# A chunked attention and maxout kernel on one core: tile 0's q and k in two halves, a new order of the first list, new planned times

## The chip, the core and the metric

The kernel runs on one core of a Trainium2 chip. Its engines work side by side: TensorE (matmuls, PE in the rows, with its weight loads as PEld), VectorE (DVE), ScalarE (ACT), GpSimd (POOL), and SyncE (SP), which issues all loads and stores here. The metric is device time in microseconds (us), the median of several runs.

## What is computed

Attention over chunks of 64 positions, for 8 batches, 8 heads, 576 positions and a head size of 64, and behind it a layer that takes the largest of three products:

```
scores = q_c @ k_c.T / 8                     per chunk of 64
attn   = softmax(scores);  x = attn @ v_c    x: 4608 tokens x 512
h      = max(x @ w1, x @ w2, x @ w3)         512 -> 768
out    = h @ w_out                           768 -> 512
```

All in float32. q and k are drawn some 6.5 times larger than v.

## The kernel before, in words

The 4608 tokens are 36 tiles of 128. **Tiles 0 to 3** are the first group, tiles 4 to 7 the second, and tiles 8 to 35 four units of 6, 8, 8 and 6. A product of float32 matrices is made of three matmuls on high and low parts (lines 175 to 177, and 587 in the units). In the units the big products are made with seven smaller products in place of eight, so sums and differences of operands ("mixing") are prepared for weights and for x.

**The steps of a tile** (`plain_steps`, line 205 on) have short names, by which the orders are written: `q` (load q and k, line 213), `v` (load v, 217), `S` (32 score matmuls, 228), `mx` (maximum, VectorE, 233), `sub` (subtract it, VectorE, 238), `exp` (ScalarE, 242), `sum`, `eps`, `rec` (VectorE, 183, 186, 189), `nrm` (normalise, 192, GpSimd or VectorE), `T` (transpose by TensorE, 254), `at` (copy of it, ScalarE, 259), `V` (32 value matmuls, 266), `xh` and `xl` (high part on ScalarE, 273, low part on VectorE, 277), or `x` (plain copy, 280). Score banks of even and odd tiles lie side by side in one tile of PSUM; buffers of e alternate between two, those of sums too.

**A piece of weights** jw (`piece`, line 122 on) is a 512 KB load `W` (142), then `A` and `B` on ScalarE (151, 156), `C` on VectorE (160), `X` (164), `H` (high part, ScalarE, 167) and `Y` (low part, 170); a `p` behind the name puts X or Y (or nrm, hl) on GpSimd.

**The first list** (`FIRST`, line 42 on) writes out the order of the first group by hand; each engine takes its own names in that order. `i7` is seven idle matmuls on zeros (756). `h00a` is the hidden product of piece 00 with the first 256 columns (tiles 0 and 1), `b` the second, `f` all 512; it is 12 matmuls and needs H and Y of its piece and xh and xl of its tiles. `F` takes the result out of PSUM, `hh` and `hl` split the hidden values, `P` and `O` are the output products and their stores, `K` stores plain weights for the units, `M` starts the planner.

**Behind M a planner sets the order.** Its clock `now` starts at -10 and moves by a step (0.6815 for three matmuls of 512 columns) with each piece of TensorE's work. `plan(at, pe, fn)` files an operation for a time, and `passed` releases what is due, in order of time; one with a `pe` moves the clock. These times set only the order in which the program gives operations to the engines. In the second group's 72 hidden steps, four insertions (`first_tiles`, `insertion`, line 857 on) put V and S of two tiles, their softmax (offsets in `SOFTMAX`) and their T between the steps; `begins` shifts the softmax of each of the two and `behind` says how long after that its transpose is due. `stores` (line 883) files the mixing of weights (GpSimd sums into `c`, high part 389, low part 392, store 406) in nine rounds of 6.94 from `MIX`. Behind the 72 steps come 24 output steps, during which `operands` (510) makes the operands X1 to X7 of unit 0, from `OPERANDS` on: differences (499), high parts on ScalarE (504), low parts on VectorE (508). Operands 4 and 5 share a room for their differences. Then unit 0 begins; its products (587) are copied out by ScalarE (601) and summed.

## Time and profile before

| what | value |
|---|---|
| median of 3 runs | 613.57 us (613.57 to 613.94) |
| the profiled execution | 613.93 us, its span 612.2 us |
| TensorE busy | 604.1 us (99%), 5107 matmuls |
| VectorE, GpSimd, ScalarE busy | 428.4 (70%), 294.0 (48%), 271.8 us (44%) |
| granted TensorE clock | 1.00 over the span |
| moved by DMA | 161.26 MB, mean 263 GB/s |

Times in the rows count from the first instruction. In a timeline each line has start, duration, engine, line of the kernel, operation, what it writes and reads, and how many instructions it merges; in brackets how long the engine stood idle before it and what ended that. A busy TensorE is not one at its peak, as ends of matmuls are modelled; starts are the surer number.

### The profile page before, as it was taken

The numbers are of one execution on the slowest core, as the hardware profiler recorded it, in microseconds if no ns is written. First come the engines' busy times: TensorE is split into PE (matmuls) and PEld (weight loads), VectorE is DVE, ScalarE is ACT, GpSimd is POOL, SyncE is SP. The second block draws the span as 40 slices with busy tenths as digits, with TensorE's granted clock in tenths as the row PEclk, the third lists the DMA queues.
The fourth block names the chain that finished last, engine by engine and source line by source line (L and its number), as shares of the span: only waits on it lengthen the run. The fifth ranks groups of instructions, "written<-read, shape, count | busy, mean of one in ns | idle before, by whom it ended". The sixth has DMA issues, their size and how long they took to land.

```text
span 612.2 us, 12724 instructions
## 1 busy us (share of the span) xinstructions
PE 604.1 (99%) x5107; PEld 526.0 (86%) x5107; DVE 428.4 (70%) x677; ACT 271.8 (44%) x483; POOL 294.0 (48%) x242
## 2 busy tenths in 40 slices
PE   8999999999999999999999999999999999999997
PEld 4888888877899999998888887888888888999997
DVE  5899834787657988794596859863868387375752
ACT  4898633444444554544252525432434252242440
POOL 3352699884257775454262624532534234242430
PEclk9999999999999999999999999999999999999999
DMA  8999729687989997889485848497565658977774
GB/s 318 385 337 307 238 103 357 231 308 276 346 290 311 358 356 267 283 303 360 175 294 172 279 152 287 144 331 285 174 204 205 200 172 265 325 247 243 241 233 177
DMA packets 54219, 161.26 MB, mean 263 GB/s; under 512 B 4880, under 2 KB 16144, under 8 KB 49168
## 3 DMA queue, kind: packets, MB, share of 16 engines
q1 hardware_dynamic: 54160, 160.45, 74.9%
q8 instruction: 40, 0.66, 0.4%
q14 instruction: 19, 0.16, 0.1%
HBM read 128.97 MB, written 31.46 MB: 262 GB/s over the span
## 4 chain that ended last, share of the span: by engine, by line
PE 77%; DVE 7%; POOL 6%; ACT 2%; issue 2%; DMA 1%; SPq 1%; POOLq 0%; ACTq 0%; DVEq 0%
PE pm L587 65%; POOL c L384 3%; PE pm L175 2%; PE pm L177 2%; PE pm L176 2%; POOL f L371 2%; DVE s L392 1%; PE y L266 1%; PE s L228 1%; DMA w<-s 1%; PE s L266 1%; ACT s L389 1%; PE y L228 1%; PE s L254 1%; DVE e L238 1%
## 5 line engine op out<-in xcount | busy, mean ns | idle before, releaser
L587 PE MATMUL pm<-X,ring 128*128 128x512 f32 (+1 forms) x1512 | 311.0, 364 | 0.3 <-ACT kept L601 0.3
L587 PEld LDWEIGHTS pm<-X,ring 128*128 128x128 f32 x1512 | 271.4, 188 | 30.6 <-ACT kept L601 0.7
L601 ACT COPY kept<-pm 128x384 f32<-128x384 f32 (+1 forms) x108 | 57.2, 534 | 139.2 <-PE pm L587 101.1
L587 PE MATMUL pm<-Y,ring 128*128 128x512 f32 (+1 forms) x504 | 103.2, 363 | 0.1
L587 PEld LDWEIGHTS pm<-Y,ring 128*128 128x128 f32 x504 | 90.6, 188 | 10.4 <-DVE Y L637 0.6
L611 POOL TENSOR_TENSOR kept<-kept 128x384 f32<-128x384 f32 (+1 forms) x36 | 45.5, 1263 | 79.9 <-ACT kept L601 79.8
L598 DVE TENSOR_TENSOR most<-pm,most 128x384 f32<-128x384 f32 (+1 forms) x72 | 44.8, 622 | 51.7 <-PE pm L587 50.3
L192 POOL TENSOR_TENSOR e<-e,sm 128x512 f32<-128x512 f32 x28 | 33.1, 1181 | 71.1 <-DVE sm L189 52.5
L175 PE MATMUL pm<-xh,wl 128*128 128x512 f32 (+1 forms) x156 | 59.8, 383 | 0.0
L177 PE MATMUL pm<-xh,wh 128*128 128x512 f32 (+1 forms) x156 | 58.3, 374 | 0.0
L176 PE MATMUL pm<-xl,wh 128*128 128x512 f32 (+1 forms) x156 | 58.2, 373 | 0.0
L607 POOL TENSOR_TENSOR kept<-kept 128x384 f32<-128x384 f32 (+1 forms) x24 | 29.7, 1236 | 57.6 <-DVE kept L604 49.1
L637 DVE TENSOR_TENSOR Y<-most,Y 128x384 fp32r<-128x384 f32 (+1 forms) x72 | 53.7, 761 | 3.4 <-ACT Y L634 3.2
L634 ACT CAST Y<-most 128x384 fp32r<-128x384 f32 (+1 forms) x72 | 40.1, 570 | 30.2 <-DVE most L598 15.9
L242 ACT ACTIVATE e<-e 128x512 f32<-128x512 f32 x36 | 22.7, 631 | 37.6 <-DVE e L238 37.5
L604 DVE TENSOR_TENSOR kept<-pm,kept 128x384 f32<-128x384 f32 (+1 forms) x36 | 22.3, 621 | 18.4 <-PE pm L587 15.2
L604 DVE TENSOR_TENSOR pm<-pm,kept 128x384 f32<-128x384 f32 (+1 forms) x48 | 30.1, 628 | 7.1 <-PE pm L587 5.7
L177 PEld LDWEIGHTS pm<-xh,wh 128*128 128x128 f32 x156 | 29.4, 188 | 5.4
L175 PEld LDWEIGHTS pm<-xh,wl 128*128 128x128 f32 x156 | 29.4, 188 | 5.1
L176 PEld LDWEIGHTS pm<-xl,wh 128*128 128x128 f32 x156 | 29.4, 189 | 4.7
L183 DVE TENSOR_REDUCE sm<-e 128x8 f32<-128x512 f32 x36 | 24.5, 680 | 8.2 <-ACT e L242 7.6
L371 POOL TENSOR_TENSOR f<-wh,wl 128x512 f32<-128x512 f32 x18 | 28.3, 1594 | 0.6
(112 smaller groups left out, 838.3 us busy)
## 6 DMA issues: line engine op xcount, KB each, us to landing
ring<-w SPq DMA_DIRECT2D x36, 1024.0 KB, 5.6
ring<-w SPq DMA_DIRECT2D x36, 768.0 KB, 5.5
ring<-wo SPq DMA_DIRECT2D x28, 768.0 KB, 4.7
buf<-in_qk SPq DMA_DIRECT2D x36, 512.0 KB, 6.4
buf<-in_vb SPq DMA_DIRECT2D x36, 256.0 KB, 4.9
w<-s SPq DMA_DIRECT2D x18, 512.0 KB, 4.0
out_t<-ao SPq DMA_DIRECT2D x16, 256.0 KB, 3.9
wo<-so SPq DMA_DIRECT2D x3, 1024.0 KB, 7.2
```

Of the source, the lines that this page charges most:

```text
L175: nc.tensor.matmul(out=o, lhsT=al, rhs=bh, start=first, stop=False)
L176: nc.tensor.matmul(out=o, lhsT=ah, rhs=bl, start=False, stop=False)
L177: nc.tensor.matmul(out=o, lhsT=ah, rhs=bh, start=False, stop=last)
L192: eng.tensor_tensor(out=e, in0=e, in1=sm.unsqueeze(2).broadcast_to([P, 8, 64]), op=ALU.mult)
L371: nc.gpsimd.tensor_tensor(out=st["f"][:, k], in0=wh[j][:, w].bitcast(F32), in1=wl[j][:, w].bitcast(F32), op=plus)
L587: nc.tensor.matmul(out=o[i], lhsT=a, rhs=b, start=new and k == 0, stop=last and k == 2, skip_group_check=i in banks_of_product)
L598: return lambda: nc.vector.tensor_tensor(out=M(k, c), in0=of(), in1=M(k, c), op=most)
L601: return lambda: nc.scalar.copy(out=kept(k), in_=o[i])
L604: return lambda: nc.vector.tensor_tensor(out=out(), in0=o[i], in1=kept(k), op=plus)
L611: (0.0, lambda: nc.gpsimd.tensor_tensor(out=kept(2), in0=kept(2), in1=kept(0), op=plus))],
L634: return lambda: nc.scalar.copy(out=y_room(i, jp)[:, 0, :half], in_=t[i]())
L637: return lambda: nc.vector.tensor_tensor(out=y_room(i, jp)[:, 1, :half], in0=t[i](), in1=y_room(i, jp)[:, 0, :half].bitcast(F32), op=minus)
```

## The change

q and k of a tile were laid out as all heads of q, then all of k. They are now laid out as heads 0 to 3 of q and k, then heads 4 to 7 of both, and tile 0 is loaded in two transfers of half the size. The hand-written list has a new order, with some X and Y moved between VectorE and GpSimd, and the planner's times have new values. The diff, without unchanged lines (the lists whole):

```diff
@@ -31,10 +31,10 @@
-SOFTMAX = (("mx", 0.93), ("sub", 1.87), ("exp", 3.09), ("sum", 3.8), ("eps", 4.34), ("rec", 4.95), ("nrm", 5.17))
+SOFTMAX = (("mx", 0.93), ("sub", 1.87), ("exp", 3.09), ("sum", 3.8), ("eps", 4.54), ("rec", 4.95), ("nrm", 5.17))
-OPERANDS = 0.94
-MIX = 0.52
+OPERANDS = 1.64
+MIX = 1.22
@@ -44,21 +44,26 @@
-i7 q0 q1 S0 i7 mx0 sub0 q2 exp0 sum0 W00 S1 A00 eps0 B00 S2 rec0 mx1 sub1 exp1 W02 nrm0p i2 C00 q3 mx2 X00p v0 i1 A02
-sum1 i8 T0 at0 S3 H00 V0 eps1 i3 rec1 sub2 nrm1p xh0 v1 mx3 exp2 T1 Y00p at1 i3 xl0 sum2 C02 V1 q4 eps2 rec2 sub3 B02
-W01 nrm2p v2 q5 xh1 X02p xl1 W10 S4 T2 exp3 A01 sum3 h00a v3 at2 eps3 rec3 V2 H02 nrm3 Y02 B01 C01 F00a W12 xh2 B10
-X01 mx4 sub4 T3 at3 H01 h02a A10 V3 Y01 S5 xh3 h01a A12 C10 W11 A11 xl3 B12 xl2 exp4 F01a F02a X10p W21 C12 W22 Z B11
-W20 hh0a W30 H10 A20 W31 Y10p h02b X12 mx5 A30 h00b q6 C20 C11 q7 B20 sum4 W42 hl0a H12 X11p Y12 X20 W32 H11 Y11 h01b
-F00b eps4 sub5 B21 H20 rec4 A21 B31 F01b F02b Y20p h10f C30 W40 B30 h12f A22 A31 C21 nrm4p exp5 C22 X30 X21 B22 h11f
-W51 H30 h20f W50 hh0b S6 C31 hl0bp H21 X31p X22 Y21 F10f H22 A32 F11f F12f v4 B51 Y30p H31 hh1f T4 h21f W41 B32 B50
-A40 Y31p sum5 mx6 A50 W62 eps5 B42 Y22p C40 h31f B40 at4 hl1f W60 C50 F20f C32 A41 X40 X32p K11 H40 F21f B41 Y40 h22f
-H32 Y32 X50 A51 C51 C41 A42 sub6 rec5 X51 H50 X41 Y50p h30f A60 h40f F22f W61 W65 W52 B62 C42 W64 H51 X42 exp6 h32f
-hh2f W63 H42 Y51 S7 H41 nrm5 B65 V4 hl2f C60 B60 Y41 F30f T5 v5 A52 X60p F31f K12 A62 F32f B52 hh3f Y42 H60 B61 C52
-hl3f F40f h41f h50f K20 sum6 C62 X52 mx7 A61 C61 xh4 F41f Y60 H52 h42f A65 X62 H62 F42f eps6 X61p Y52p v6 A64 Y62 h51f
-H61 hh4f A63 P30 Y61p P20 sub7 B63 C63 K00 rec6 exp7 hl4f P32 sum7 P31 F50f nrm6p P21 X63p at5 eps7 H63 Y63p rec7 P10
-xl4 nrm7p V5 K22 K01 B64 F51f K10 T6 xh5 h52f v7 at6 C64 P22 X64p C65 P00 xl5 T7 F52f H64 hh5f P23 X65p P01 hl5fp M
-at7 H65 P11 V6 V7 q8 q9 P12 xh6 xh7 xl6 P02 Y64 P13 xl7 Y65 P33 P34 P14 P35 P24 P03 P25 P04 K21 O2 P15 P05 K02 O0 O3
-O1
+q0 q1 i5 S0 mx0 i3 q2 S1 W01 mx1 sub0 exp0 i7 i2 v0 sub1 exp1 sum0 eps0 v1
+rec0 A01 W00 sum1 B01 S2 nrm0p mx2 i8 eps1 C01 A00 T0 rec1 at0 sub2 exp2 sum2 eps2 C00
+q3 B00 nrm1p i5 V0 T1 xh0 rec2 X01p S3 xl0 at1 nrm2p W10 H01 mx3 V1 Y01p sub3 A10
+xh1 exp3 X00p xl1 i1 sum3 T2 q4 B10 S4 eps3 v2 W02 rec3 h01a at2 q5 v3 V2 nrm3
+H00 A02 W12 Y00 T3 B02 xh2 C02 X02 at3 H02 h00a mx4 F00a W20 C10 Y02 V3 xh3 F01a
+S5 A12 B12 X10p xl3 W11 H10 xl2 C12 Z X12 B11 A11 h02a W21 W32 h00b Y10p F02a H12
+W22 sub4 C11 A20 hh0a C20 h02b W40 W30 exp4 hl0a B20 A21 h01b X20 B21 X11 W60 F00b W52
+W41 C21 Y12p sum4 eps4 H20 H11 B32 X21 B30 h10f Y11 F01b A32 Y20p A30 rec4 H21 C32 F02b
+hh0b C30 nrm4p mx5 hl0bp A22 Y21 B41 h12f W42 W63 v4 F10f q6 X32 C22 sub5 B22 h11f A42
+X22p W31 h20f h21f B40 X30 H32 Y32 S6 F11f H22 H30 T4 F12f B42 hh1f W51 mx6 A31 C42
+Y22p B52 X42 A40 exp5 C31 at4 Y30p W50 hl1f H42 h22f W61 Y42p A41 h30f B31 h32f F20f C41
+X31p A60 sub6 X41p F21f B51 H31 C40 Y31 H41 exp6 F22f sum5 h42f h31f hh2f sum6 A52 X40 Y41p
+B50 H40 eps5 B60 W62 A50 eps6 C60 B63 C52 hl2f X52p C50 rec5 q7 F30f Y40p A51 h41f h40f
+F31f F32f S7 B61 hh3f H52 K12 X60 C51 X51p W64 nrm5 B64 K01 X50 hl3f Y52 F40f A62 rec6
+F41f C62 F42f H50 V4 T5 xh4 nrm6p Y50 mx7 B62 A64 H51 X62p H60 hh4f xl4 v5 at5 h52f
+Y51 sub7 W65 Y60 exp7 A63 C64 h50f h51f sum7 H62 C63 eps7 X63p A61 P00 Y62 hl4f V5 T6
+C61 H63 F50f X61 F51f H61 K00 A65 rec7 F52f Y61p P20 P22 K11 hh5f v6 X64 P30 C65 P32
+P31 xh5 H64 K22 K20 at6 P21 Y63p nrm7p xl5 hl5fp P01 B65 v7 P10 P23 K10 T7 X65 M
+at7 H65 P11 V6 V7 q8 q9 P12 xh6 xh7 xl6 P02 Y64 P13 xl7 Y65 P33 P34 P14 P35
+P24 P03 P25 P04 K21 O2 P15 P05 K02 O0 O3 O1
@@ -208,9 +213,13 @@
-            st["r"] = att.tile([P, 2, 8, 64], F32, name="buf", tag=("raw", "kk", "aa")[t % 3] if t < 8 else ("raw", "kk")[t % 2],
+            st["r"] = att.tile([P, 2, 2, 4, 64], F32, name="buf", tag=("raw", "kk", "aa")[t % 3] if t < 8 else ("raw", "kk")[t % 2],
-            nc.sync.dma_start(out=st["r"], in_=qk[t])
+            if t == 0:
+                for k in range(2):
+                    nc.sync.dma_start(out=st["r"][:, k], in_=qk[t][:, 512 * k:512 * k + 512])
+            else:
+                nc.sync.dma_start(out=st["r"], in_=qk[t])
@@ -225,7 +234,7 @@
-                    nc.tensor.matmul(out=s[b, c, g, :], lhsT=r[a, 0, 2 * g + h, :], rhs=r[a, 1, 2 * g + h, :],
+                    nc.tensor.matmul(out=s[b, c, g, :], lhsT=r[a, g // 2, 0, g % 2 * 2 + h, :], rhs=r[a, g // 2, 1, g % 2 * 2 + h, :],
@@ -409,8 +418,8 @@
-                (0.12, sum_of(0, sums(1), a11, minus)), (4.07, sum_of(2, a11, a21, minus)),
-                (3.79, sum_of(3, a12, sums(0), minus)), (4.86, high), (5.79, low), (8.77, mixed)]
+                (2.32, sum_of(0, sums(1), a11, minus)), (4.07, sum_of(2, a11, a21, minus)),
+                (3.79, sum_of(3, a12, sums(0), minus)), (4.86, high), (5.79, low), (7.57, mixed)]
@@ -465,9 +474,9 @@
...
@@ -508,20 +517,20 @@
-            return [(0.0, high(1)), (0.39, low(1)), (2.71, mix(5, b12, b11, nc.vector)), (3.48, high(5)),
-                    (3.31, mix(6, b22, source[5], nc.vector)), (8.01, mix(7, b22, b12, nc.gpsimd)), (3.37, high(6)),
-                    (7.69, low(6)), (7.41, high(2)), (7.89, low(5)), (10.85, mix(4, b21, source[6], nc.gpsimd)), (7.67, low(2)),
+            return [(0.0, high(1)), (0.0, low(1)), (2.01, mix(5, b12, b11, nc.vector)), (3.83, high(5)),
+                    (3.31, mix(6, b22, source[5], nc.vector)), (8.21, mix(7, b22, b12, nc.gpsimd)), (3.37, high(6)),
+                    (7.49, low(6)), (7.06, high(2)), (7.89, low(5)), (12.35, mix(4, b21, source[6], nc.gpsimd)), (8.37, low(2)),
-            return [(1.17, high(3)), (2.45, low(3)), (0.47, high(4)), (1.08, low(4))]
+            return [(1.17, high(3)), (1.75, low(3)), (1.0, high(4)), (1.08, low(4))]
...
@@ -606,16 +615,16 @@
...
@@ -640,20 +649,20 @@
...
@@ -687,13 +696,13 @@
...
@@ -847,14 +856,14 @@
-            plan(at + 2.27, 0.0, lambda: steps(n)["at"]())
+            plan(at + 1.92, 0.0, lambda: steps(n)["at"]())
-            plan(at - loads + 0.38 * k, 0.0, lambda n=n: steps(n)["v"]())
-            plan(at + 1.41 + 0.58 * k, 0.0, lambda n=n: steps(n)["x"]())
+            plan(at - loads + 0.03 * k, 0.0, lambda n=n: steps(n)["v"]())
+            plan(at + 1.41 + 0.78 * k, 0.0, lambda n=n: steps(n)["x"]())
@@ -863,11 +872,11 @@
-        gap = (time - lead - 0.5) / (len(own) - 1)
+        gap = (time - lead - 0.0) / (len(own) - 1)
-            insertion(values, scores, now + lead + gap * i, 11.6, nc.gpsimd if last else nc.vector,
-                      (0.7, 4.6) if last else (0.2, 3.02), (10.9, 10.9) if last else (10.1, 9.4))
+            insertion(values, scores, now + lead + gap * i, 12.25, nc.gpsimd if last else nc.vector,
+                      (2.2, 3.9) if last else (0.0, 3.12), (11.25, 8.7) if last else (9.3, 9.4))
@@ -878,7 +887,7 @@
...
@@ -887,7 +896,7 @@
...
@@ -920,7 +929,7 @@
...
@@ -941,13 +950,13 @@
-              ("do", lambda: tiles(1, 4 * JT * STEP + span(0))), ("do", lambda: load(0, 0, 1.72, 1.35)), ("do", lambda: load(0, 1, 2.31, 5.13))]
+              ("do", lambda: tiles(1, 4 * JT * STEP + span(0))), ("do", lambda: load(0, 0, 2.02, 2.15)), ("do", lambda: load(0, 1, 2.31, 5.83))]
-        parts.append(("do", lambda u=u: operands(u + 1, 7.76)))
+        parts.append(("do", lambda u=u: operands(u + 1, 7.86)))
@@ -994,8 +1003,8 @@
-    qk, vb = (np.concatenate([a.transpose(0, 1, x, 2, y).reshape(NT, P, 512) for a in group], axis=2)
-              for group, x, y in (((q, k), 4, 3), ((v,), 3, 4)))
+    qk = np.stack([a.transpose(0, 1, 4, 2, 3).reshape(NT, P, 2, 256) for a in (q, k)], axis=3).reshape(NT, P, 1024)
+    vb = v.transpose(0, 1, 3, 2, 4).reshape(NT, P, 512)
```

## Rows read from the trace of the kernel before

**Rows 1.** Waits of TensorE: us in total, times, longest us

```profile
PE x L266 <- DMA buf<-in_vb: 1.3, 1, 1.3
PE s L228 <- DVE e L238: 0.7, 1, 0.7
PE y L266 <- ACT xs L259: 0.4, 1, 0.4
PE pm L587 <- ACT kept L601: 0.3, 1, 0.3
PE s L254 <- DVE e L192: 0.3, 1, 0.3
```

**Rows 2.** Line 213, its first two loads: duration ns, first and last start; landing

```profile
L213 SPq DMA_DIRECT2D buf<-in_qk x2: 388/402/416, 0.7 to 1.2; - x2
...
DMA to landing us min/median/max: 3.9/4.3/4.7
```

**Rows 3.** Timeline of the first 25 us; columns as told above

```profile
4.70 0.56 PEld L228 LDWEIGHTS s<-buf 64*64 64x64 f32 x32 [0.99 <-DMA buf<-in_qk]
...
5.47 0.69 DVE L233 TENSOR_REDUCE mx<-s 128x8 f32<-128x512 f32 x1 [4.07 <-PE s L228]
...
7.58 0.69 DVE L183 TENSOR_REDUCE sm<-e 128x8 f32<-128x512 f32 x1 [0.70 <-ACT e L242]
...
14.35 0.69 DVE L277 TENSOR_TENSOR xl<-x,xh 128x512 fp32r<-128x512 f32 x1 [1.16 <-ACT xh L273]
...
16.90 0.69 PE L228 MATMUL s<-buf 64*64 64x64 f32 x32 [0.67 <-DVE e L238]
...
16.92 0.69 DVE L277 TENSOR_TENSOR xl<-x,xh 128x512 fp32r<-128x512 f32 x1
...
17.96 0.36 PE L175 MATMUL pm<-xh,wl 128*128 128x256 f32 x1
...
18.30 0.59 ACT L259 COPY xs<-tp 128x512 f32<-128x512 f32 x1 [0.20 <-PE tp L254]
...
18.79 0.62 ACT L167 CAST wh<-ao 128x512 fp32r<-128x512 f32 x1
...
19.56 0.69 PE L266 MATMUL x<-xs,buf 64*64 64x64 f32 x32
...
22.96 0.56 PEld L228 LDWEIGHTS s<-buf 64*64 64x64 f32 x32 [0.20 <-DVE e L238]
...
23.59 0.39 PE L175 MATMUL pm<-xh,wl 128*128 128x256 f32 x1
```

**Rows 4.** Timeline of VectorE (normalisation) and TensorE (transpose), third insertion

```profile
143.42 0.69 DVE L192 TENSOR_TENSOR e<-e,sm 128x512 f32<-128x512 f32 x1
...
144.33 0.60 PE L254 MATMUL y<-ident,e 128*128 128x128 f32 x4
```

**Rows 5.** Timeline of TensorE: the values of the fourth insertion

```profile
149.99 0.69 PE L266 MATMUL y<-xs,buf 64*64 64x64 f32 x32 [0.38 <-ACT xs L259]
```

**Rows 6.** Timeline behind the loop: VectorE, ScalarE, TensorE, GpSimd

```profile
146.69 0.68 DVE L317 TENSOR_TENSOR m<-pm,m 128x512 f32<-128x512 f32 x1
...
156.57 0.83 ACT L504 CAST X<-stage 128x768 fp32r<-128x768 f32 x1 [2.16 <-DMA w<-s]
...
161.71 0.60 PE L254 MATMUL y<-ident,e 128*128 128x128 f32 x4
...
164.01 1.05 POOL L192 TENSOR_TENSOR e<-e,sm 128x512 f32<-128x512 f32 x1 [3.01 <-DVE sm L189]
```

**Rows 7.** Timeline at unit 0's begin: VectorE, GpSimd, ScalarE

```profile
166.14 1.53 DVE L508 TENSOR_TENSOR X<-stage,X 128x768 fp32r<-128x768 f32 x1 [2.30 <-ACT X L504]
...
169.63 2.35 POOL L499 TENSOR_TENSOR most<-stage,most 128x768 f32<-128x768 f32 x1 [2.77 <-ACT xs L259]
...
172.01 0.84 ACT L504 CAST X<-most 128x768 fp32r<-128x768 f32 x1 [2.83 <-POOL most L499]
...
173.97 1.24 ACT L601 COPY kept<-pm 128x384 f32<-128x384 f32 x3
```

More of the change, by code (lines that the diff above doesn't have):

```diff
@@ L467, in store_out @@
         a11, a12, a21, a22 = part(0, 0), part(0, 1), part(1, 0), part(1, 1)
-        return [(0.28, whole(0)), (2.76, whole(1)), (3.98, sum_of(2, a21, a22, plus, True)),
-                (6.03, sum_of(0, sums(2), a11, minus)), (5.88, sum_of(1, a11, a21, minus)),
-                (8.56, sum_of(3, a12, sums(0), minus)), (12.4, high), (13.55, low), (17.02, mixed)]
+        return [(0.0, whole(0)), (1.26, whole(1)), (3.28, sum_of(2, a21, a22, plus, True)),
+                (5.03, sum_of(0, sums(2), a11, minus)), (5.18, sum_of(1, a11, a21, minus)),
+                (8.21, sum_of(3, a12, sums(0), minus)), (12.4, high), (13.55, low), (16.02, mixed)]
     turns = [0, 0]
@@ L607, in fourth @@
                 nc.gpsimd.tensor_tensor(out=kept(1) if w else M(1, 1), in0=kept(3), in1=kept(1), op=plus)
-            after = {1: [(0.17, copy(1, 0))], 5: [(0.46, copy(5, 1))],
+            after = {1: [(0.27, copy(1, 0))], 5: [(0.56, copy(5, 1))],
                      6: [(0.0, copy(6, 2)),
-                         (0.0, lambda: nc.gpsimd.tensor_tensor(out=kept(2), in0=kept(2), in1=kept(0), op=plus))],
+                         (0.35, lambda: nc.gpsimd.tensor_tensor(out=kept(2), in0=kept(2), in1=kept(0), op=plus))],
                      7: [(0.0, sum_to(7, 0, lambda: kept(3))), (0.72, fourth)],
@@ L655, in hidden @@
                     product(o, i, hi, lo, X[i][:, 0, k, :half], X[i][:, 1, k, :half], k == 0, k == 1)
-                    last = [(0.3, loads[i == 4])] if i in (5, 4) else []
+                    last = [(0.2, loads[i == 4])] if i in (5, 4) else []
                     yield STEP_H[count], after[i] + last if k else []
@@ L689, in project @@
                              2: lambda: store(m, (0, 0), lambda out, m=m: nc.scalar.copy(out=out, in_=o[m][2])),
-                             6: lambda: [(0.0, copy(m, 6, 2)), (1.52, second(m))],
+                             6: lambda: [(0.0, copy(m, 6, 2)), (1.82, second(m))],
                              7: lambda: [(0.0, lambda m=m: sum_of(m, 7, 0)(kept(m)))],
@@ L695, in project @@
                     if m:
-                        after += [(1.51, fn) for fn in loads[p]]
+                        after += [(2.21, fn) for fn in loads[p]]
                     for jp in range(3):
@@ L880, in tiles @@
         for i, (values, scores) in enumerate(zip(own, nexts)):
-            insertion(values, scores, now + lead + gap * i, 18.05, nc.gpsimd, (0.9, 0.74 + 0.28 * gap), (10.73, 10.73))
+            insertion(values, scores, now + lead + gap * i, 17.55, nc.gpsimd, (0.9, 0.74 + 0.28 * gap), (11.33, 10.73))
     def stores():
@@ L889, in stores_plain @@
         for jp in range(3):
[L890 removed]
+            plan(now + 28.1 + 15.95 * jp, 0.0, lambda jp=jp: store_plain(jp))
     def change():
@@ L921, in loads_within, with last_operands @@
         return [[fn] if fn else [] for fn in behind]
-    def last_operands(u, begin=0.1):
+    def last_operands(u, begin=0.5):
         if u < len(units):
```

25 lines of the change are left out of this document (12 added, 13 removed).

## Prediction

> **What bounds the kernel now.** I read the waits of TensorE first [rows 1]. In 612.2 us its stream stands still in few places, and the list is short because the engine is fed nearly everywhere: 1.3 us for the first v, 0.7 us for a subtraction, and 0.3 to 0.4 us in three places further on. So the order of the work on the other engines can bring only three things: a start of full feeding earlier than now, the few stalls behind it, or new stalls. No matmul is added or removed, and the seven runs of idle products hold 31 matmuls before and after.
>
> Then the timeline of the start [rows 3]. The first scores begin at 4.70, when tile 0 has landed, and the first hidden product stands at 17.96. From the third one (23.59) on TensorE is fed. VectorE is the engine that works through this stretch: its first maximum is at 5.47, and the low part of tile 1, the last thing that a hidden product of two tiles needs from attention, is at 16.92 and ends at 17.61. In those 12.14 us VectorE stands still for 0.70 before the first sum and 1.16 before the first low part. The second of these comes from the v of tile 0, for which the value product waited 1.3 us [rows 1, 3].
>
> **The change at the start.** Ahead of the first hidden product the new list has the same TensorE work (S0 to S4, T0 to T2, V0, V1), and on VectorE the same 21 operations up to xl1, in another order, with C01 and C00 for C00 and C02. So only the idle time of VectorE and its first moment differ.
>
> The split. The first transfer is issued at 0.7 and lands 3.9 later, at 4.66; the second is issued at 1.2 and lands 4.7 after its issue, at 5.9 [rows 2]. Two of 512 KB therefore land 1.2 apart, though their own times overlap, and half a tile is worth 0.6. The first half should land at 4.05, the second at 4.66, and half of S0 is done by then. S0 takes 0.77 from 4.70 to the maximum at 5.47; with half left, mx0 starts some 0.24 earlier, at 5.23. The extra issue costs SP about 0.4 (its row), behind which q1 waits, but q1 is still held by the data ahead of it: I cost that at nothing. If that cover were gone, q1 would land 0.4 later and S1 with it.
>
> The order. S4 stood 0.67 us for a subtraction that reads the other half of its banks [rows 3]: a score product waits for every reader of the pair of banks that stands before it in the list. In the new list mx1 stands ahead of sub0, so VectorE waits for S1, which needs q1 (5.9) and the end of mx0 (5.23 + 0.69 = 5.92). With S0's 0.77 behind a handover of 0.06, mx1 starts at 6.75: 0.83 idle. The 0.24 of the split are worth having only because q1 lands no later than mx0 ends. Next, sub2 needs the bank of e that T0 reads, and T0 stands behind eight idle products: 0.2. Then sum2 waits for its exponential with nothing between, 0.70, as sum0 does now. Last, xl1 waits for xh1, which ScalarE has behind H01 and A10: about 0.7. The v of tile 0 stands behind four whole transfers of 512 KB instead of six, so V0's 1.3 and the 1.16 behind it go. New idle 0.83 + 0.2 + 0.7 + 0.7 = 2.4 against 1.86: xl1 ends at 17.61 - 0.24 + 0.54 = 17.9, and some of it comes back because neighbours on VectorE that don't depend on each other overlap. I take 17.85 for the first hidden product, against 17.96.
>
> Up to the third hidden product TensorE needs 1.60 (17.96 to 19.56) and 4.03 (to 23.59) less the 0.2 that S5 waited: 5.43, so 23.28 if nothing waits, 0.3 before 23.59. What could wait is the word H02, behind nine ScalarE operations after xh1. They start as close as 0.49 apart (18.30 to 18.79) and last up to 0.69. At 0.57 they end at 22.1, its low part at 22.8, and nothing waits. At 0.68 they end at 23.6, the low part at 24.3, and three VectorE operations of 0.6 on, the low parts of tiles 2 and 3 at 26.1, where the first 'b' product now could start at 25.03. So the start is worth from -0.6 (nothing waits, xl1 at 17.6) to +1.0. I take **-0.3**, since the rows show these engines overlapping.
>
> **The loop's planned times.** A planned time only sets a place in an engine's queue, and a TensorE insertion moves by whole steps. The planner's clock stands at 0.904 at the loop (-10 and 16 steps of 0.6815 behind M), and each inserted item adds its own cost. I worked this out for the insertions at which rows 1 show a wait or where little slack is left.
>
> The first transpose of the third insertion was due at 40.61 + 0.2 + 10.1 = 50.91 and is due at 40.94 + 0 + 9.3 = 50.24; 6.74 of insertions stand before it, so it came behind step (50.91 - 7.64) / 0.6815, the 64th, and now the 63rd: a step of 0.68 earlier. It stands at 144.33, and its normalisation ended at 143.42 + 0.69 = 144.11 [rows 4]. A slack of 0.22 can't pay 0.68: **+0.46**. Behind it stands only a step of matmuls; its copy on ScalarE is used 5 us later. In the second insertion the same transpose moves two steps; rows 1 show no wait for it and I cost that at nothing, or at up to 0.7 if its slack is as thin.
>
> The fourth V goes from 56.04 to 56.54, behind step 71 instead of 70. It waits 0.38 for ScalarE [rows 5], and one more step covers that: **-0.38** (nothing, if ScalarE's copy moves along with it).
>
> Behind the loop, the transposes of the last two tiles stood behind steps 84 and 90 (due 67.64 and 71.54) and both go behind 87 (69.99 and 69.14), the later tile's first. The first stood at 161.71, so both are due at some 161.71 + 3 x 0.68 = 163.8. The normalisation of the later tile, on GpSimd at 164.01, ended at 165.06 [rows 6]. VectorE's work ahead of it is as long as before, and its start is set by the cast of operand 1 at 156.57, which waited for the store of the last mixed weights to land: if that lands as now, TensorE waits 1.3 here, with the remaining output steps and unit 0 queued behind it. But that store hangs on a maximum of hidden products at 146.69 (line 317), behind the second normalisation of the third insertion; it was due 0.03 behind it, and goes 0.4 ahead of it (48.83 against 49.23), and with it a cast, the last high part, low part and store, by up to 1.2. Between 0 and +1.3 I take **+0.4**, nearer to the end at which the maximum goes first, since that order is certain.
>
> At the first step of unit 0, TensorE waits 0.3 for a copy on ScalarE. That copy (173.97) stands behind the cast of operand 4 at 172.01, which waited 2.83 for GpSimd's subtraction at 169.63, and this for the low part of operand 5 [rows 7], because both share one room. VectorE did low 2 first (due at 0.94 + 7.67 = 8.61, and waiting at 166.14 for ScalarE), then low 6 (8.63) and low 5 (8.83). Now low 6 is due at 1.64 + 7.49 = 9.13, low 5 at 9.53 and low 2 at 10.01: low 5 no longer stands behind that wait, the subtraction can come some 2 us earlier, and the copy up to 0.8 sooner. **-0.4**, between 0 and -0.5.
>
> The rest (the mixing's sums, loads of the rings, the offsets in the units' sums and casts) I cost at nothing: the mixing keeps its order on GpSimd, and TensorE waits for none of these in rows 1. If that cover goes, each is a stall like those shown, 0.3 to 0.7 once.
>
> The sum is -0.3 + 0.46 - 0.38 + 0.4 - 0.4 = **-0.2**. The profiled execution took 613.93 (a span of 612.2 and 1.7 around it), so 613.7 for it; against the median of the runs, 613.57, it gives **613.4**.
>
> **A rule against the split.** Rows 2 say that two queued transfers overlap: they land 1.2 apart, not 3.9. The Trainium skill (DMA: Bandwidth & Descriptors, "Rules for kernel authors") advises one large transfer over several small ones, and its section on the anatomy of a DMA gives about 2 us fixed for each on another path; if that were paid in series the start would be about 2 later by an estimate from that page. No run here yet shows two halves of a tile.
>
> **The rivals.**
> Faster: everything at the short end. Start -0.6, the transposes at 144 and 164 don't wait because VectorE comes sooner, V -0.38, unit 0 -0.5: -1.5, so 612.1. For it speaks that each of these places waits for an engine that has idle time beside it; against it that all have to go well.
> Slower: the two transposes behind the loop. Their place is the 163.8 of the output stage; it decides when the later tile's normalisation ends after that, and it costs 1.3 with the store landing as now. With the 0.46, the V and the start at nothing and unit 0's copy still waiting, 613.57 + 1.8 = 615.4; with the start at its long end another 1.0. For it speaks that the chain of GpSimd, cast, store and cast had no slack before.
> The split does harm: the second half starts only when the first has landed and needs its own 2 to 4 us. S0 would then end 2 later, 615.6.
> The split does nothing: mx1 waits for q1 in any case, and if q1 lands 0.4 later for the extra issue, the 0.24 is gone. 613.7, inside the forecast's own range.
>
> **How the numbers follow.** A measurement of this kernel can tell about 0.2%, 1.2 us, from no change. The forecast with its own unknowns (and the last rival in it) gets 0.5; the faster rival 0.27; the slower one 0.2; the harmful split 0.03. So faster 0.27, same 0.5, slower 0.23. The range leaves out the far halves of both outer cases: 611.6, half a microsecond under the faster rival for a stall that the small shifts may take away, to 615.4, the slower one without the start's long end.
>
> **What would show it.** In the profile after, S0 begins near 4.1 and the first maximum near 5.2; V0 doesn't wait for a v; VectorE waits 0.8 for S1; the first hidden product stands at 17.6 to 18.3, the third near 23.3. In the loop a transpose near 144 waits about 0.5 for a normalisation, and V at 150 for nothing. Near 164 two transposes stand one behind the other, and the first waits up to 1.3 for GpSimd. In unit 0 low 6 and low 5 stand before low 2, and no copy is waited for. The prediction is wrong if the third hidden product comes after 24, if a wait of over 0.7 us stands anywhere behind 25 but near 164, or if the units' loops, untouched in my sum, differ in length.

## The result and the profile after

The changed kernel takes **617.8 us** (median of six runs, 615.5 to 618.9), the kernel before in the same rounds 613.5: ratio 1.0068, interval 1.0056 to 1.0081. It is slower by 0.7%, above the range. The profiled execution took 616.23 us with a span of 614.4.

The waits of TensorE after (us in total, times, longest), against [rows 1]:

```profile
PE s L237 <- DMA buf<-in_qk: 1.6, 1, 1.6
...
PE x L275 <- ACT xs L268: 0.6, 1, 0.6
PE pm L596 <- DMA ring<-wo: 0.5, 1, 0.5
PE s L263 <- DVE e L197: 0.5, 1, 0.5
PE pm L596 <- DVE Y L646: 0.3, 1, 0.3
```

The wait for the first v is gone, as are those for the copies of xs at 150 and of kept at 174. New at the top is a score block that waits for q and k, and new in the loops is a product that waits for pieces of w_out.

The loads of tile 0 (line 220) and of tile 1 (line 222), against [rows 2]:

```profile
L220 SPq DMA_DIRECT2D buf<-in_qk x2: 386/401/416, 0.7 to 1.2; - x2
...
DMA to landing us min/median/max: 3.0/3.1/3.2
...
L222 SPq DMA_DIRECT2D buf<-in_qk x1: 424/424/424, 1.6 to 1.6; - x1
...
DMA to landing us min/median/max: 6.3/6.3/6.3
```

The halves land at 3.73 and 4.35, a little ahead of the 4.05 and 4.66 of the sum. q1, issued at 1.65, lands at 7.98; before, it was at 5.87.

The timeline of the start after, against [rows 3]:

```profile
3.77 1.32 PE L237 MATMUL s<-buf 64*64 64x64 f32 x32
...
5.16 0.69 DVE L242 TENSOR_REDUCE mx<-s 128x8 f32<-128x512 f32 x1 [3.77 <-PE s L237]
...
8.12 0.69 PE L237 MATMUL s<-buf 64*64 64x64 f32 x32 [1.63 <-DMA buf<-in_qk]
...
8.87 0.69 DVE L242 TENSOR_REDUCE mx<-s 128x8 f32<-128x512 f32 x1 [3.02 <-PE s L237]
...
19.39 0.39 PE L180 MATMUL pm<-xh,wl 128*128 128x256 f32 x1
...
24.81 0.39 PE L180 MATMUL pm<-xh,wl 128*128 128x256 f32 x1
```

The first score block and maximum come early, as the split promised. Then VectorE stands still for 3.02 us, since the second maximum is next in its order and S1 waits for q1. The first hidden product is 1.43 later than before, the third 1.22. The profile records the higher level of the granted clock (2.4 GHz) from 6.45 on (before, from 4.54 on), so S0 still runs at the lower one (1.2 GHz) and takes 1.32, while S1 takes 0.69.

Timelines of the loop after: the transposes near 145 and 165 with their normalisations, the fourth values, the cast of operand 1, and the new stall, against [rows 4 to 6]:

```profile
144.59 0.68 DVE L197 TENSOR_TENSOR e<-e,sm 128x512 f32<-128x512 f32 x1
...
145.64 0.60 PE L263 MATMUL y<-ident,e 128*128 128x128 f32 x4
...
152.16 0.69 PE L275 MATMUL y<-xs,buf 64*64 64x64 f32 x32
...
155.49 0.83 ACT L513 CAST X<-stage 128x768 fp32r<-128x768 f32 x1 [0.56 <-DMA w<-s]
...
163.44 1.04 POOL L197 TENSOR_TENSOR e<-e,sm 128x512 f32<-128x512 f32 x1 [1.30 <-PE pm L182]
...
165.21 0.60 PE L263 MATMUL s<-ident,e 128*128 128x128 f32 x4
...
266.87 1.80 PE L596 MATMUL pm<-Y,ring 128*128 128x384 f32 x9 [0.54 <-DMA ring<-wo]
```

Neither the transposes nor the values wait: the normalisations end at 145.27 and 164.48, ahead of their transposes. The product at 266.87 stands for a load.

In what follows "lost" is the time from one matmul's start to the next one's, above what the same pair takes elsewhere. By it, the loop before lost 0.45 at 130 (T), 0.54 at 149 (V), 0.50 at 174 (copy of kept) and 0.30 at 375 (Y). After, it loses 0.33 at 120 (V), 0.61 at 132, 0.71 at 266 (load), 0.26 at 277 (sums) and 0.50 at 377: 2.41 against 1.79, so in this execution **0.6 of the loss is in the loops**. The rest is the start. For it one profile of before is too few: first hidden products in the nine profiles with the old list and undivided loads, here and below, stand at 17.14 to 18.16, median 17.4. Against that, 19.39 is **2.0 late**. Together 2.6, and this execution's 616.23 is 2.8 above the 613.4 of the kernel before in most rounds. It is the second fastest of the six; what a slower one loses besides is seen in e15.

### The profile page after: what moved, and what is told of

Same layout as the page of the kernel before. It is cut to its first block, busy times and chain, and to the rows that moved or that the text cites. A ratio compares the mean times of both kernels' runs of the same rounds, so it can differ in the third digit from the quotient of the medians.

```text
span 614.4 us, 12712 instructions
## 1 busy us (share of the span) xinstructions
PE 605.8 (99%) x5107; PEld 526.5 (86%) x5107; DVE 434.0 (71%) x677; ACT 271.5 (44%) x483; POOL 298.9 (49%) x242
## 4 chain that ended last, share of the span: by engine, by line
PE 90%; DVE 5%; DMA 2%; ACT 1%; issue 1%; POOL 1%; SPq 0%; DVEq 0%; POOLq 0%
PE pm L596 63%; PE pm L180 6%; PE pm L181 6%; PE pm L182 6%; PE s L237 2%; PE s L275 1%; PE y L275 1%; DMA ring<-wo 1%; DMA buf<-in_qk 1%; PE y L237 1%; PE s L263 1%; PE y L263 1%; PE pm L765 1%; PE tp L263 1%; POOL c L393 1%
## 5 line engine op out<-in xcount | busy, mean ns | idle before, releaser
L646 DVE TENSOR_TENSOR Y<-most,Y 128x384 fp32r<-128x384 f32 (+1 forms) x72 | 52.3, 746 | 5.7 <-ACT Y L643 5.7
```

The costliest lines, as they stand in the source:

```text
L646: return lambda: nc.vector.tensor_tensor(out=y_room(i, jp)[:, 1, :half], in0=t[i](), in1=y_room(i, jp)[:, 0, :half].bitcast(F32), op=minus)
```

## The experiments

Each was timed beside the kernel before. All ratios are to it (613.1 to 613.4 there); "h" is the first hidden product and "q1" its landing, in the profile.

| run | what | us | ratio (interval) | h | q1 |
|---|---|---|---|---|---|
| e1 | split alone | 614.39 | 1.0019 (1.0011 to 1.0028) | 18.65 | 7.88 |
| e2 | list alone | 615.01 | 1.0029 (1.0018 to 1.0041) | 19.93 | 5.75 |
| e3 | times alone | 614.52 | 1.0022 (1.0012 to 1.0032) | 17.17 | 5.75 |
| e4 | change, no split | 616.50 | 1.0055 (1.0042 to 1.0068) | 19.56 | 5.91 |
| e5 | list, old idle runs | 614.20 | 1.0015 (1.0006 to 1.0023) | 18.09 | 5.71 |
| e6 | list, mx1 later | 615.20 | 1.0024 (1.0015 to 1.0034) | 20.10 | 5.93 |
| e7 | times, old load | 614.17 | 1.0011 (1.0002 to 1.0019) | 17.41 | 5.56 |
| e8 | split by partitions | 615.17 | 1.0024 (1.0014 to 1.0035) | 19.60 | 8.02 |
| e9 | before, short idle runs | 613.81 | 1.0011 (1.0002 to 1.0020) | 17.62 | 5.85 |
| e10 | change, three undone | 615.07 | 1.0033 (1.0021 to 1.0046) | 18.14 | 5.64 |
| e11 | operands' times | 613.57 | 1.0007 (0.9998 to 1.0016) | 17.86 | 5.81 |
| e12 | the same, last insertion later | 613.44 | 1.0005 (0.9996 to 1.0014) | 17.22 | 5.70 |
| e13 | insertions' times | 615.45 | 1.0029 (1.0017 to 1.0041) | 17.30 | 5.79 |
| e14 | times but those and the load | 614.51 | 1.0017 (1.0008 to 1.0025) | 17.14 | 5.75 |
| e15 | change again | 616.85 | 1.0054 (1.0032 to 1.0075) | 20.64 | 8.03 |
| e16 | split, q1 between | 615.71 | 1.0029 (1.0016 to 1.0041) | 20.12 | 5.72 |
| e17 | last insertion later | 616.90 | 1.0054 (1.0042 to 1.0066) | 18.16 | 5.81 |

### The change in its three parts

e1 is the kernel before with the new layout and the two transfers, e2 with the new list, e3 with the new planned times, e4 the changed kernel with one transfer:

```diff
 # e1 (the new layout beside it is left out here), and taken back in e4
-            nc.sync.dma_start(out=st["r"], in_=qk[t])
+            if t == 0:
+                for k in range(2):
+                    nc.sync.dma_start(out=st["r"][:, k], in_=qk[t][:, 512 * k:512 * k + 512])
+            else:
+                nc.sync.dma_start(out=st["r"], in_=qk[t])
```

> The kernel before with the new layout and tile 0 in two transfers, old list, old times. Theory A (the two half transfers disturb the stream of loads behind them): S0 begins near 3.8, but q1 lands near 8.0 instead of 5.9, S1 waits for it, the first hidden product comes about 1 us later than 17.96, and the time is 0.5 to 2 us above the kernel before. Rival B (the new list's order costs the start, the split is harmless): q1 lands at 5.9, the first hidden product within 0.3 of 17.96, the time within 0.5 us of before.

> The kernel before with the new first list alone: one transfer for tile 0, old layout, old times. Theory A: q1 lands at 5.9, S1 does not wait beyond 6.2, the first hidden product stands at 17.6 to 18.3, no loss at the start, and the time is within 1 us of before. Rival B: the first hidden product comes after 19 although q1 is on time, and the time is 1.5 us or more above before.

> The kernel before with the new planned times alone: old list, old layout. Theory C (the times cost about 1 us in the loops, by the outer weights that land late near 266, by a transpose near 132 and an operand near 377, less what they save at unit 0 and at the fourth insertion): a wait of TensorE for the outer weights near 266 of about 0.5, no wait for a ScalarE copy at 174, and 0.5 to 1.5 us above before. Rival: the times are neutral (within 0.4 us of before) and the whole difference is made in the first 25 us.

> The changed kernel with tile 0 in one transfer (new layout, list and times kept). Theory A: q1 lands at 5.9 and S1 starts near 6.2, so the start gains 1.5 to 2 us against the changed kernel, and its runs scatter less: 614 to 616. Rival B: no gain, 617 to 618, with the same scatter.

The parts cost 1.05, 1.67 and 1.18 over the kernel before, 3.9 of the 4.3: each loses by itself. In e1 the split moves q1 to 7.88 and the start by 1.2 against the usual one. What the split costs inside the change is not shown by the times: e4's median is 1.3 below the changed kernel's in the first rounds, 0.35 below it in e15, and the intervals overlap. And e4's start is no earlier than the changed kernel's, so the list holds the start too, with q1 on time. The timeline of e2 shows how:

```profile
5.65 1.46 PE L761 MATMUL pm<-h 128*128 128x512 bf16 x3
...
7.04 1.14 PE L233 MATMUL s<-buf 64*64 64x64 f32 x32
...
8.25 0.69 DVE L238 TENSOR_REDUCE mx<-s 128x8 f32<-128x512 f32 x1 [1.77 <-PE s L233]
8.51 3.02 PE L761 MATMUL pm<-h 128*128 128x512 bf16 x8 [0.33 <-issue]
...
11.47 0.69 PE L233 MATMUL s<-buf 64*64 64x64 f32 x32
...
12.09 1.90 PE L761 MATMUL pm<-h 128*128 128x512 bf16 x8
13.83 0.60 PE L259 MATMUL tp<-ident,e 128*128 128x128 f32 x4
```

A score block lasts 1.14 at 7.04 and 0.69 at 11.47, and eight idle products 3.02 and then 1.90. The profile records the higher level of the granted clock from 10.8 on only, that of before from 4.5 on. The eight idle products stand ahead of S2 in TensorE's order, so they hold it back to 11.47. e4 shows the same; its higher level comes at 9.9:

```profile
7.18 1.14 PE L233 MATMUL s<-buf 64*64 64x64 f32 x32
...
8.65 2.52 PE L761 MATMUL pm<-h 128*128 128x512 bf16 x8 [0.33 <-issue]
```

So in e4 the late clock takes the place that the late q1 has in the first profile of the change, where the clock is high before S1.

### The list's start: the clock or VectorE's order

e5 gives the list its old idle runs back; e6 moves mx1 behind sub0 and exp0; e9 puts the short idle runs into the old list:

```diff
 # e5, against e2
-q0 q1 i5 S0 mx0 i3 q2 S1 W01 mx1 sub0 exp0 i7 i2 v0
+i7 q0 q1 S0 i7 mx0 q2 S1 W01 mx1 sub0 exp0 i7 i2 v0
 # e6, against e2
-S1 W01 mx1 sub0 exp0 i7 i2 v0
+S1 W01 sub0 exp0 mx1 i7 i2 v0
 # e9, against the kernel before
-i7 q0 q1 S0 i7 mx0 sub0 q2
+q0 q1 i5 S0 mx0 i3 sub0 q2
```

> The kernel before with the new first list, but with the old list's idle products in the head of TensorE's order (i7 ahead of S0 and i7 ahead of S1, where the new list has i5 and i3). Theory D: the new list costs the start because TensorE has too little to do ahead of S1, so its clock is granted later (the idle products stood 0.43 us apart until 10.8 in the list-alone run, in the kernel before only until 4.5). It expects the idle products to be 0.22 apart by 7 and the first hidden product back from 19.93 to 18.2 or earlier, and a time of about 613.4 (0 to 0.6 above the kernel before). Theory E: it is the order on VectorE alone, mx1 ahead of sub0, which makes sub0, exp0 and all behind them wait for S1. It expects the clock to rise early and the first hidden product still at 19.3 or later, the time within 0.4 of the list-alone run's (1.6 above the kernel before).

> The kernel before with the new first list, its short idle runs kept, but with mx1 moved behind sub0 and exp0, so that VectorE no longer waits for S1 before it goes on with tile 0. Theory D (the late clock): the clock still rises only near 10, S1, S2 and T0 are as late as in the list-alone run, and the first hidden product stays at 19.3 or later; the time stays about 1.6 above the kernel before. Theory E (VectorE's order): sub0 is done near 7.5 instead of 10, so rec0 and nrm0 come some 1.2 earlier, the first hidden product near 18.5, and the time within 0.6 of the kernel before's.

> The kernel before, its list and all, with nothing changed but the idle products in the head of TensorE's order: i5 and i3 where it has i7 and i7. No work on VectorE, ScalarE or the queues moves. Theory D (the late clock): the 1.2 GHz level lasts past 8 us, with the idle products 0.43 apart and the score blocks at 1.13, and the first hidden product goes from 17.96 to 19.0 or later; the time is 0.8 to 1.8 above the kernel before's, ratio 1.0013 to 1.0030. Rival: idle products are only there to fill waiting time, and to take six away ahead of S1 costs nothing: first hidden product by 18.2 and a ratio within 1.0008 of 1.

The timeline of e5 stands against that of e2:

```profile
6.81 0.69 PE L233 MATMUL s<-buf 64*64 64x64 f32 x32
...
7.57 0.69 DVE L238 TENSOR_REDUCE mx<-s 128x8 f32<-128x512 f32 x1 [1.55 <-PE s L233]
7.66 1.89 PE L761 MATMUL pm<-h 128*128 128x512 bf16 x8 [0.16 <-issue]
...
9.51 0.69 PE L233 MATMUL s<-buf 64*64 64x64 f32 x32
...
11.94 0.66 PE L259 MATMUL tp<-ident,e 128*128 128x128 f32 x4
```

With the old idle runs the clock is high before S1, S2 comes 1.96 earlier, T0 1.89 and the first hidden product 1.84. So the late clock is the larger part of what this list alone costs at the start, 1.84 of 2.5. (In time e5 is 0.8 above the kernel before and e2 1.7, but the intervals overlap.) The changed kernel's first profile stands 1.31 behind e5 at S1 (8.12 against 6.81) and 1.30 at the first hidden product: there the late q1 is the whole difference. In the old list a late clock costs the start little: in e9 too it rises late (8.6), the idle runs are as short, and the first hidden product stands at 17.62. There sub0 and exp0 run while S1 is late:

```profile
5.87 0.69 DVE L233 TENSOR_REDUCE mx<-s 128x8 f32<-128x512 f32 x1 [4.47 <-PE s L228]
...
6.60 0.69 DVE L238 TENSOR_TENSOR e<-s,mx 128x512 f32<-128x512 f32 x1
...
7.34 1.55 PEld L228 LDWEIGHTS s<-buf 64*64 64x64 f32 x64 [1.05 <-DVE e L238]
```

So theory D fell for the old list: a first hidden product at 19.0 or later was expected, and the time is 0.4 above the kernel before's, not 0.8 to 1.8. (Its rival's ratio, within 1.0008, was missed too: 1.0011.) e6 did not test what it was made for. S1 stood ahead of sub0 in the list, and sub0, which reads the same pair of banks, waited for S1 itself:

```profile
8.44 0.69 DVE L243 TENSOR_TENSOR e<-s,mx 128x512 f32<-128x512 f32 x1 [1.77 <-PE s L233]
```

VectorE's 1.77 moved from one operation to the next. With q1 on time and the clock high, e5 still stands at 18.09 against the usual 17.4, and its time, 0.8 above the kernel before, agrees with these 0.7. VectorE's order is the likely cause, since sub0 starts at 8.18 there and at 6.60 in e9, but that is argued: no run moves S1 itself behind sub0 in the new list.

### Why q1 is late

e8 cuts tile 0 by partitions, so that a row in a transfer keeps its 4 KB; e16 issues q1 between the two halves:

```diff
 # e8, against e1
-  nc.sync.dma_start(out=st["r"][:, k], in_=qk[t][:, 512 * k:512 * k + 512])
+  nc.sync.dma_start(out=st["r"][64 * k:64 * k + 64], in_=qk[t][64 * k:64 * k + 64])
 # e16: tile 0 issues half 0, tile 1 its own transfer and then half 1 (only tile 1's lines)
+  nc.sync.dma_start(out=st["r"], in_=qk[t])
+  if t == 1:
+      second.pop()()
```

> The kernel before with the new layout and two transfers for the first tile, but cut by partitions (64 each, 4 KB in a row) instead of by columns (128 partitions, 2 KB in a row each), so S0 has to wait for both. Theory A1: what delays q1 to 7.9 in the split run is its half-size packets (2 KB), which keep the sixteen DMA engines out of step. It expects q1 to land by 6.3, S0 near 4.7 and the first hidden product within 0.3 of the kernel before's 17.96, so a time within 0.4 of it. Theory A2: it is the second transfer itself. It expects q1 to land at 7.3 or later here too, and the first hidden product 0.5 or more later than in the kernel before.

> The split run's kernel (the kernel before with the new layout and two transfers for the first tile), with one thing moved: q1 is issued between the two halves instead of behind both, so it is the second transfer in SP's queue again and the second half the third. Theory A3 (place): what the third transfer of the queue lands at is 7 to 8, whatever its size (6.9 to 7.9 in the runs without the split, 7.9 to 8.0 for q1 in the four with it), the second's 4.3 to 5.9. It expects q1 to land by 6.0 and the second half at 6.3 or later, 1.5 or more behind the split run's 4.8, so S0 ends at 6.5 or later. Theory A4 (bytes): the transfers share the engines and land as their bytes are through, so moving 256 KB from ahead of q1 to behind it lets q1 land some 0.6 earlier than in the split run, near 7.3, and the half some 1.2 later, near 6.0.

In e8 q1 lands at 8.02, so the size of the packets is not the cause. In e16 it is second in the queue and lands at 5.72, as before the change; the half behind it lands at 6.36. TensorE's wait for it:

```profile
6.40 0.71 PE L235 MATMUL s<-buf 64*64 64x64 f32 x16 [1.15 <-DMA buf<-in_qk]
```

So q1 is late as the third transfer. The third of the queue lands at 6.9 to 7.9 in the runs without a split (7.1 before, 7.9 in e7), and q1 as third at 7.88 to 8.03 in all four with the two halves ahead, though only 512 KB instead of 1 MB stand ahead of it. The place alone doesn't set the landing, since e16's third, the half, lands at 6.36; nor do the bytes by theory A4, which had q1 near 7.3 there and the half near 6.0. What was moved says more; by stretches up to q1's landing, with the DMA's GB/s in the last column, the changed kernel and then the kernel before:

```profile
1.00:7.98 6.98, 5.03 (x40) 1.90 (x40) 1.09 (x2) 1.01 (x1) 0.45 (x2) 1.00 0.79 279
```

```profile
1.00:5.87 4.87, 4.33 (x42) 1.75 (x43) 0.80 (x2) 1.01 (x1) 0.45 (x2) 1.00 0.79 283
```

That is 1.95 MB against 1.38, where q1 and all ahead of it are 1.05. So q1 did not wait for its turn in bytes: some 0.9 MB of the loads behind it were moved before its last packet landed, 0.33 before the change. Why some of its packets come so late stays open. But in e16 the scores of tile 0 wait 1.15 for their second half, the clock rises at 10.7, and the first hidden product is the later of the two: neither order of the three transfers helps.

### The loop's times

e7 is e3 with one number of `project` taken back. e10 is the changed kernel with the three causes found by then undone:

```diff
 # e7, and in e10
-                        after += [(2.21, fn) for fn in loads[p]]
+                        after += [(1.51, fn) for fn in loads[p]]
 # e10 too: one transfer for tile 0 (e4), idle runs i7 and i7 (e5)
```

> The kernel before with the new planned times, all but one: the loads of project() keep their old 1.51 where the change has 2.21. Theory C: the stall of a product behind a load of w_out pieces at 264.12 (0.85 lost in the run of the times alone, none in the kernel before) is that number's, since it puts the load one place later in SP's queue. It expects that stall gone, the others of the times alone as they were (T at 129.7 0.6, Y at 375 0.5), and a time 0.6 to 0.9 below the times-alone run's: 613.4 to 614.0, the ratio to the kernel before 0.9995 to 1.0010. Rival: the load is late whatever its place, by the traffic that the other new times put ahead of it: the stall stays at 0.4 or more and the time stays above 614.1.

> The changed kernel with the three causes found so far taken back: one transfer for the first tile, the idle products i7 and i7 in their old places, the loads of project() at 1.51. All the rest of the new list and of the new planned times stays. If these three are the loss, the first hidden product comes by 18.3, the stall near 265 is gone, and the time falls by 1.3 (split) + 1.9 (start) + 0.85 (load) = 4.0 from 617.8 to 613.4 to 614.4, ratio 0.9995 to 1.0015. Rival: there is a fourth cause, spread over the loop's new times or the list's later part, which the sums of the single runs (617.8 - 1.3 - 0.8 - 0.4 = 615.3) point to: the time stays at 615 or above, ratio 1.0020 or more.

The waits of TensorE in e3, which e7 answers to:

```profile
PE pm L587 <- DMA ring<-wo: 0.7, 1, 0.7
PE s L254 <- DVE e L192: 0.5, 1, 0.5
```

In e7 the first of them is gone, and of the other stalls only one of 0.27 in a score block at 136, so that number is the stall's cause. The time fell by 0.35 only, less than the 0.85 lost there; e7's first scores of tile 2 waited 0.6 for a load that landed at 7.9. e10 stays at 615.07. Its profile says where: the start is 0.7 late, and the stalls lose 3.2 against 1.8, 2.1 together, which is what its 615.48 has above 613.4. For its other runs (614.5 to 616.2) nothing is shown. The largest of the stalls is new (1.37 lost):

```profile
PE y L233 <- issue: 1.2, 1, 1.2
```

It lies in the middle of a score block at 136 and waits for nothing that the profile shows. e3 lost 0.27 in the same block, the changed kernel nothing. What it is stays open. The trace has a fetch of instructions (queue q8, 16 KB) from 135.1 to 136.0 just ahead of it, where e3, e7 and the change have theirs at 133.2 to 134.3; that TensorE stood for it is not shown.

The planned times were then cut in two. e13 has the insertions' numbers alone (eps, the copies behind transposes, loads and copies of v, spacing, `begins` and `behind`), e14 all the others but the load's. e11 has only the operands' and e12 and e17 move the last insertion of the loop half a microsecond, with and without these:

```diff
 # e11, and in e12
-OPERANDS = 0.94
-MIX = 0.52
+OPERANDS = 1.64
+MIX = 1.22
 # and the fourteen offsets of operands()
 # e12 and e17
-            insertion(values, scores, now + lead + gap * i, 11.6, nc.gpsimd if last else nc.vector,
+            insertion(values, scores, now + lead + gap * i + (0.5 if last else 0.0), 11.6, nc.gpsimd if last else nc.vector,
```

> The kernel before with only the first unit's operands at the new times (the two constants of their start and the fourteen offsets of operands()), which were picked for the stall at 173.83 (0.50 lost behind a copy of kept on ScalarE). If the order of the operands is that stall's cause it goes or falls under 0.2, nothing else changes, and the time is 0.3 to 0.6 below the kernel before's, ratio 0.9990 to 0.9998. Rival: the stall went in the times-alone run because the copies themselves were planned later (0.17 to 0.27, 0.46 to 0.56): it stays at 0.35 or more, ratio 0.9997 to 1.0006.

> The operands run's kernel, and besides the last insertion of the first loop half a microsecond later (one step of the loop), which takes its V product behind the copy of xs that it waits for at 149.23 (0.54 lost). If both stalls are placed right, the profile shows neither, and the time is 0.7 to 1.1 below the kernel before's, ratio 0.9982 to 0.9990: the version that beats both kernels. Rival: the step behind it moves the wait to the next insertion's transposes (up to 0.5 near 164), and the time stays within 0.3 of the operands run's.

> The kernel before with only the numbers of the attention tiles' insertions at the new values: eps in the softmax's times, the copies behind the transposes, the loads and copies of v, the even spacing of the first loop's insertions, their begins and lags, the units' 17.55 and 11.33. Theory G (the fourth cause lies here): the run with the load's number taken back still stood 0.7 above the kernel before although its stalls summed to nothing against it; the transposes near 130 wait longer (0.6 to 0.9 instead of 0.45), the values near 118 too (0.25), and score blocks stop for want of instructions in some executions (1.37 lost at 136.07 in the mended run's profile, for nothing that the profile shows), against 0.54 won at 149. It expects a time 0.4 to 1.0 above the kernel before's, ratio 1.0006 to 1.0016, and single runs above 615. Rival H: these numbers are worth what their stalls say, 0.54 won less 0.4 lost: ratio 0.9994 to 1.0004, no single run above 614.8.

> The kernel before with all the new planned times but the insertions' numbers and the load's: operands, their sums and stores, the copies of the first unit, the units' work on VectorE and GpSimd, the late operands. Theory G: what is left is only the stall at 173.83 won (0.50) and those at 275 and 375 lost (0.26 and 0.2): ratio 0.9992 to 1.0004. Rival H: the loss is in these: the products near 275 and 375 wait for VectorE, ratio 1.0006 or more.

> The kernel before with only the last insertion of the first loop half a microsecond later, without the operands' new times. Its V product then stands one step of the loop behind and the wait at 149.23 (0.54 for a copy of xs) goes or falls under 0.25; the other stalls stay as they are (0.45 at 130, 0.50 at 174, 0.30 at 375). Expected: 0.2 to 0.5 below the kernel before's, ratio 0.9991 to 0.9998, the version that beats both. Rival: the step only moves the wait to the transposes behind it near 164, or the same wait stays, as in the run with the operands: ratio 0.9997 to 1.0008.

None of them beats the kernel before. e11 takes the stall at 174 away, as its theory had it: GpSimd's subtraction comes 1.35 earlier than before and the cast behind it waits 1.09 instead of 2.83 [rows 7].

```profile
168.28 2.44 POOL L499 TENSOR_TENSOR most<-stage,most 128x768 f32<-128x768 f32 x1 [0.95 <-PE s L254]
...
170.76 0.83 ACT L504 CAST X<-most 128x768 fp32r<-128x768 f32 x1 [1.09 <-POOL most L499]
```

But T at 130 then loses 0.86 and V at 149 0.96, about twice what they did. MIX moved with the operands and puts the mixing's low parts at other places among VectorE's softmax operations; that this is the reason was not tried by itself. e12 takes 0.66 of that back at 149 and is level with the kernel before. e14 shows the same pair (0.90 and 0.99). e13 and e17 show waits of the kind that the prediction feared, at transposes: the third insertion's in e13, then e17's behind the loop and the copy in unit 0:

```profile
144.03 0.82 DVE L192 TENSOR_TENSOR e<-e,sm 128x512 f32<-128x512 f32 x1
...
145.00 0.63 PE L254 MATMUL y<-ident,e 128*128 128x128 f32 x4 [2.00 <-DVE e L192]
```

```profile
168.41 0.66 PE L254 MATMUL s<-ident,e 128*128 128x128 f32 x4 [1.50 <-POOL e L192]
...
177.64 0.62 PE L587 MATMUL pm<-X,ring 128*128 128x384 f32 x2 [1.32 <-ACT kept L601]
```

With the new insertions and the old mixing, T stands 2.00 us for its normalisation; with both new, as in e3, e7 and the change, it doesn't wait. So neither half stands without the other: alone they cost 2.2 and 1.3, together 0.7 (e7), and with the load's number 1.2 (e3). The two transposes behind the loop don't wait in e13. e17's wait there is another case: it keeps the old offsets and moves the whole insertion.

### The changed kernel again

```diff
 # e15: no edit
```

> The changed kernel once more, for a second profile and more single runs. All theories expect 617 to 618.5, q1 landing at 7.5 or later, the first hidden product at 19.0 to 20.5 and the stall near 266. Whether q1's late landing belongs to the two transfers or was that run's chance: if q1 lands by 6.3 here it was chance.

q1 lands at 8.03 again, and the first hidden product is at 20.64, 1.25 later than in the first profile. A view of e15 by stretches (busy us of each engine, and PEclk, the granted clock):

```profile
4.40:7.60 3.20, 1.22 (x20) 0.54 (x19) 0.69 (x1) 0.00 (x0) 0.00 (x0) 1.00 0.97 350
7.80:11.00 3.20, 2.84 (x37) 1.65 (x38) 1.65 (x3) 0.33 (x1) 0.00 (x0) 0.50 1.01 394
11.20:14.00 2.80, 2.80 (x43) 1.45 (x42) 2.63 (x9) 2.50 (x5) 1.04 (x1) 1.00 1.02 419
```

TensorE stood 2.07 us for q1, until 8.16, and in that wait, at 7.7, the clock fell from the higher level to the lower, until 11.1. So here the late q1 and a low clock add up. Single runs of the change lie between 614.4 and 618.9, those of the kernel before mostly within 612.3 to 614.3. That the late q1 makes the start less steady is not shown: e1, with q1 as late, lies within 613.6 to 615.3. This profile sums as the first does: start 3.2, stalls 0.9 more than before, 4.1 of the 4.3 by which its 617.67 exceeds 613.4.

## Why the prediction was wrong

**"Held by the data ahead of it: I cost that at nothing", or 0.4 if that cover went.** This step failed first. The halves did land one behind the other, 0.6 apart (1.0 to 1.4 in e1, e8 and e15), S0 began at 3.77 and mx0 at 5.16, near what was worked out. But q1 lost 2.1, not 0.4, by becoming the third in the queue (e1, e8; e16 puts it back and it lands at 5.72). That is worth 1.05 us of time in e1, and 1.3 at the first hidden product in the change (against e5). The data ahead of it, the two halves, had landed by 4.35, 3.6 before q1, so it was no cover. The rival of a harmful split had the right sign and the wrong transfer: it made the second half late. The rule that I weighed, one large transfer rather than several (the Trainium skill, DMA: Bandwidth & Descriptors, "Rules for kernel authors"), agrees with e1 in the sign. A fixed cost in series between the halves did not show; the next load paid.

**"I take -0.3" for the start.** This failed most: it cost 2.0 to 3.2. I counted VectorE's idle time and took 0.83 for S1. It was 3.02 with q1 late, 1.77 with q1 on time and the clock low (e2, e4), and 1.55 in e5 with the clock high, as S1 stood at 6.81 behind seven idle products and not right behind mx0. The terms for sub2 and sum2, 0.2 and 0.7, came as 0.35 and 0.69; the one for xl1 did not come. And the seven idle runs were counted, 31 before and after, but not where they stand or at which clock they run: in the list alone, with five and three ahead of S1, the lower level reaches to 10.8, and eight idle products hold S2 (e2, e5). In the change this is paid where the clock is low behind S1, as in e15, not in the first profile. Of the signs that I had set, the third hidden product after 24 came true at 24.81, and the units' loops differ in length (0.71 at 266).

**T of the third insertion, +0.46, and the two transposes near 164, +0.4.** Neither came. The first is real when only the insertions move (2.00 in e13): the step's shift was right, and it failed by holding VectorE's work ahead of it as it was, while the other planned times, MIX among them, moved too (e7). Near 164 the short end of the range came true: the cast of operand 1 stands at 155.49 after a wait of 0.56 for the store, where it was at 156.57 after 2.16, and the later normalisation ends 0.73 ahead of its transpose. Whether the maximum's place or MIX did this was not separated: nothing waits there in e13 either, but TensorE comes there 2.8 later than in e3, behind its stall. A smaller loss, 0.16, came at 132 instead.

**The fourth V, -0.38, and unit 0's copy, -0.4.** Both right: 0.54 and 0.50 won. e11 confirms the second's cause, with the subtraction 1.35 earlier where I had said some 2.

**"The rest ... I cost at nothing."** Failed: 0.71 at the load of `project` (its cause by e7), 0.26 at 277, 0.20 more at 377 and 0.33 at 120, 1.5 in all. "A stall of 0.3 to 0.7 once" was the right size; I gave it no place in the sum.

The slower rival's mechanism, the transposes near 164, did not happen; the time went past its 615.4 by the start and the load.

## What to carry to other kernels

When a load is split or added, follow every transfer behind it in its queue to its reader, not only the split one. Idle matmuls are work in TensorE's order: price them at the clock that the profile shows there, and look at what stands behind them. Offsets that set queue places act in groups; price a shift with the others already moved, since here two halves that lose 2.2 and 1.3 alone lose 0.7 together.
